# Values of batch 1 issued after the last keys of batch 0 have landed: a fused attention and expert kernel on one core

## The chip, the cores and the metric

The kernel runs on one core of one Trainium2 chip. The metric is the time of one execution on the device in microseconds (us); the kernel before takes 200.95 us, the median of 3 runs (200.51 to 201.13).

## What is computed

Attention over pooled keys and values, then a mixture of experts on its output. There are 8 batches, 8 heads, 576 rows of queries, keys and values with 64 columns, and 8 experts (512 to 1024 to 512).

```python
k_p = k.reshape(B, H, Sp, pool, D).mean(axis=3)      # pool = 8, Sp = 72
v_p = v.reshape(B, H, Sp, pool, D).mean(axis=3)
scores = scale * np.matmul(q, k_p.transpose(0, 1, 3, 2))
attn = softmax(scores)
x = np.matmul(attn, v_p)                             # to rows of 512
...
logits = xn @ en.T / tau                             # cosine router
expert_idx = np.argmax(logits, axis=1)
h = np.maximum(x[mask] @ w1[e], 0.0)                 # for each expert e
out[mask] = gate_w[mask, None] * (h @ w2[e])
```

## The kernel before

Each of the 8 batches goes through the same steps, and the steps of several batches run beside each other on the engines. Keys (`K`), values (`V`) and queries (`Q`) of a batch are loaded and cast to 16 bits by DMAs that GpSimd issues, 576 KB each as they land: `load_rows` (line 319) for keys and values, `load_q` (line 325) for queries. A load of keys or values has 72 rows of partitions. For batch 0 keys and values come in two DMAs each, 64 rows and then the last 8: `V0.0`, `V0.1`, `K0.0`, `K0.1`, and the queries in two halves, `Q0.0` and `Q0.1`. The values' mean gives a guess of the expert that the batch will use (`GM`, `GC`, `GL`, `GD`); `PK` reads that guess into a register of GpSimd (line 359), and then the expert's weights are loaded, 1024 KB each: `W1b` (line 343) and `W2b` (line 349). In the names the first digit behind the letters is the batch, except for weights: W10 is the first weight matrix for batch 0, W20 the second.

VectorE halves the values and keys three times (lines 448, 455, 462: `VA`, `VB`, `KA`, `KB`). For batch 0 alone TensorE sums the keys instead (line 472). VectorE transposes the queries (line 548), TensorE makes the scores (line 589), ScalarE the exponentials (597), TensorE the products with the values (634), VectorE normalizes (369, 370), TensorE transposes the result (378), then come the router and the two products with the weights (707, 719, 726). Matmuls of ones (814) keep TensorE at work in between early on. SyncE issues the stores of the output.

The order is not written by hand: `Plan.order` simulates the engines and the 16 DMA engines once, when the kernel is built, and picks the step that can start first; `TUNED` shifts priorities. For the loads the order is fixed by the list `LOADS`. Its beginning:

```python
LOADS = """
V0.0 V0.1 K0.0 K0.1 Q0.0 Q0.1 V1 PK0 W10 K1 Q1.0 W20 V2 PK1 W11 K2 Q2.0 V3 W21 V4 K3 PK2 W12
...
ROWS_DMA, Q_DMA, W_DMA = (12, 4.0, 1.2), (16, 2.85, 1.2), (16, 5.0, 2.2)
```

The second line of constants is the planner's own table of transfers: how many DMA engines a load of 72 rows, of queries and of weights is spread over, and the time that it assumes. The chosen order is emitted step by step. Each engine then runs its own instructions in that order, and waits on semaphores for data and for free buffers. There are two buffers each for keys, values and queries. All loads go through one software queue that GpSimd fills; the DMA engines work through it in order.

Some stores already wait for a late load on purpose: `note` records the instruction of a load under its name in `landing`, and `store` makes the store wait for it (`BEHIND`).

Of the kernel before, what the change touches and what calls it, by code (L numbers as in the profile page):

```python
# [106 lines left out]
class Plan:  # L107
# [5 lines left out]
    def add(self, name, engines, busy, prio, run, after=(), takes=(), uses=(), late=0.0,  # L113
            mode=None, tail=0.0):
        if isinstance(engines, str):
            engines = (engines,)
        if not isinstance(busy, tuple):
            busy = (busy,) * len(engines)
        s = Step(name, engines, busy, late, prio + TUNED.get(name, 0.0), [a for a in after if a], list(takes),
                 list(uses), run, mode, tail)  # L120
        for b in s.takes + s.uses:
            b.left += 1
        self.steps.append(s)
        self.by_name[name] = s
        return name
# [88 lines left out]
def kernel(  # L214
# [94 lines left out]
    def at_load(name):  # L309
        return -1000.0 + loads.index(name)  # L310
# [3 lines left out]
    def wire(dma, share=1.0):  # L314
        k, took, first = dma
        return k, took * share, first

    def load_rows(a, b, raw, g0=0, g1=G):
        return nc.gpsimd.dma_start(
            out=raw.rearrange("p h t d -> p h (t d)")[g0:g1],  # L320
            in_=a[b].rearrange("h (g t) d -> g h (t d)", g=G)[g0:g1])

    def load_q(b, qq, h0, n):
# [4 lines left out]
    landing = {}  # L328
    behind = dict(zip((f"S{t}" for b in range(B) for t in
                       [f"T{b}.{c}" for c in range(4)] + [f"L{b}"]), BEHIND))  # L330
    tails = {load: 0.34 if t[1] == "L" else 0.68 for t, load in behind.items()}

    def note(name, load):
        landing[name] = load.ins.name

    def store(name, eng, o, y):
        st = eng.dma_start(out=o, in_=y)
        if name in behind:
            tc.add_manual_dep(st.ins, landing[behind[name]], mybir.DependencyInfo(
                mybir.DependencyClass.Sync, mybir.DependencyReason.DATA), reason="late store")  # L340

    def load_w1(e_val, w1, cond=None):
        return nc.gpsimd.dma_start(
# [64 lines left out]
    def attention(b, base, xt):  # L408
# [3 lines left out]
        n = lambda s, *i: s + str(b) + "".join(f".{j}" for j in i)  # L412
# [4 lines left out]
        for c, src, raw in (("V", v, vr), ("K", k, kr)):  # L417
            if b == 0:
                add(n(c, 0), 'POOL', 0.9, at_load(n(c, 0)),
                    lambda src=src, raw=raw: load_rows(src, b, raw.tile, 0, 64),  # L420
                    takes=[raw], mode=(16, 2.78 if c == "V" else 2.7, 1.2), late=0.9)
                add(n(c, 1), 'POOL', 0.6, at_load(n(c, 1)),
                    lambda src=src, raw=raw: load_rows(src, b, raw.tile, 64),
                    uses=[raw], mode=(8, 1.25 if c == "V" else 0.3, 1.2), late=0.9)
            else:
                add(n(c), 'POOL', 0.8, at_load(n(c)),
                    lambda c=c, src=src, raw=raw: note(n(c), load_rows(src, b, raw.tile)),
                    takes=[raw], mode=wire(ROWS_DMA), tail=tails.get(n(c), 0.0), late=0.9)
        if b == 0:
            for i in range(NQ):  # L430
                add(n("Q", i), 'POOL', 0.8, at_load(n("Q", i)), lambda i=i: load_q(b, qq, i, 1),
                    takes=[] if i else [qq], uses=[qq] if i else [], mode=(16, 1.3 + i, 1.2), late=0.9)
        else:
            add(n("Q", 0), 'POOL', 0.8, at_load(n("Q", 0)), lambda: note(
                n("Q", 0), load_q(b, qq, 0, NQ)),
                takes=[qq], mode=wire(Q_DMA), tail=tails.get(n("Q", 0), 0.0), late=0.9)
# [30 lines left out]
        if b == 0:  # L467
# [14 lines left out]
            for a in range(NQ):  # L482
# [5 lines left out]
                    late=0.12)  # L488
# [3 lines left out]
        if b:  # L492
            add(n("KA"), 'DVE', 1.14, pr(-0.2), lambda: halve(kr.tile, 4),
                [n("K")] + (["XM0.4"] if b == 1 else []), uses=[kr],
                late=0.1)
            add(n("KB"), 'DVE', 1.08, pr(-0.2), k_fold, [n("KA")], takes=[kp], uses=[kr],
                late=0.1)
# [75 lines left out]
        else:  # L573
# [5 lines left out]
                late=0.1)  # L579
# [45 lines left out]
        for c in range(NC):  # L625
# [28 lines left out]
            def square(c=c, x=x):  # L654
# [9 lines left out]
                late=0.12)  # L664
# [77 lines left out]
    def ffn(b, base, xt):  # L742
        n = lambda s, *i: s + str(b) + "".join(f".{j}" for j in i)
        w1, w2 = Buf(w1_r[b % NW]), Buf(w2_r[b % NW])
        P = PERIOD
        add(n("PK"), 'POOL', 1.4, at_load(n("PK")), lambda: pick(b), [n("GD")])
        add(n("W1"), 'POOL', 0.8, at_load(n("W1")), lambda: note(
            n("W1"), load_w1(chosen[b], w1.tile, other(b))), [n("PK")], takes=[w1], mode=wire(W_DMA, 1.0 if b < NW else 1.0 - 1.0 / E), tail=tails.get(n("W1"), 0.0), late=0.9)
        add(n("W2"), 'POOL', 0.8, at_load(n("W2")), lambda: note(
# [21 lines left out]
        for c in range(4):  # L771
            p, y = Buf(bank, psum), Buf(y_r)
            f = base + P * (8 + 2 * c) / 17.0
            add(n("Y", c), 'PE', 1.73, f,
                lambda c=c, p=p: y_mm([h.tile for h in hT], w2.tile, c, p.tile[:, 0:DM]),
                [n("W2")] + hs,
                takes=[p], uses=[w2] + hT, late=0.22)
            add(n("YE", c), YE_ON, YE_BUSY, f - 2.0,
                lambda c=c, p=p, y=y: scale_rows(
                    y.tile, p.tile[:, 0:DM], g[:, c:c + 1], plan.by_name[n("YE", c)].on),  # L780
                [n("Y", c), n("ND")], takes=[y], uses=[p], late=0.12)
            add(n("ST", c), 'SP', 0.1, f, lambda c=c, y=y: store(
                n("ST", c), nc.sync, chunk_rows(o_b, c), y.tile), [n("YE", c), behind.get(n("ST", c))],
                uses=[y], mode=(0 if n("ST", c) in behind else 16, 0.68, 1.2), late=0.9)
# [19 lines left out]
    def put_last(o_b, y, name=""):  # L804
        for r in range(2):
            eng = nc.scalar if r and name == f"SL{B - 1}" else nc.sync
            store(name, eng, last_rows(o_b)[r], y[ts(r, 64), 0:DH])
# [171 lines left out]
    for b in range(B):  # L979
        xt = Buf(xt_r)  # L980
        attention(b, b * PERIOD, xt)
        ffn(b, (b + 1) * PERIOD, xt)
# [104 lines left out]
```

## Time and profile before

| | before |
|---|---|
| time, median of 3 | 200.95 us |
| the profiled execution | 201.33 us |
| its span, first to last instruction | 199.7 us |
| TensorE / VectorE / ScalarE / GpSimd busy | 95% / 70% / 68% / 22% |
| DMA moved | 38.71 MB, 194 GB/s over the span |

The profile is of one execution. Times in its rows are us from the start of the span. PE is TensorE's matmul, PEld its loading of weights, DVE VectorE, ACT ScalarE, POOL GpSimd, SP SyncE; a q behind an engine is its sequencer, which waits, reads registers and issues. L319 is line 319 of the kernel. Buffers' numbers are left out, so that `vr` is any buffer of raw values, `kr` of keys, `qq` of queries, `w` of weights. A matmul's end is modelled, so that neighbours seem to overlap.

### The profile page before, as it was taken

What the parts mean: (1) busy time and instruction counts of PE and PEld (TensorE: products, weight loads), DVE (VectorE), ACT (ScalarE), POOL (GpSimd) and SP (SyncE); (2) the same over time, 40 slices, a digit from 0 to 9 for tenths busy, and PEclk for the clock granted to TensorE, in tenths of its full rate; (3) what the DMA queues carried; (4) which work ended last, traced back from release to release, by engine and by line L of the source; (5) the groups of instructions that cost most, each with busy time, mean ns of one, the idle gap of its engine ahead of it and who ended that gap; (6) DMA issues with size and microseconds to landing.
All of it is one profiled execution on the core that took longest, in us unless ns stands there. A gap on an engine that the chain in (4) does not pass through costs nothing.

```text
span 199.7 us, 5353 instructions
## 1 busy us (share of the span) xinstructions
PE 188.9 (95%) x2080; PEld 124.1 (62%) x2081; DVE 140.1 (70%) x409; ACT 136.6 (68%) x313; POOL 43.0 (22%) x59
## 2 busy tenths in 40 slices
PE   7969999999999999999999999999999999999970
PEld 5854687547864676468666567566655677578430
DVE  2274699749997995688997997879997468241600
ACT  4016886768896979759867778469957988468430
POOL 7434025232204321035003500133000600002000
PEclk9999999999999999999999999999999999999997
DMA  3999999999999999999999999999997599990051
GB/s 49 172 191 199 207 211 197 195 200 205 210 188 190 214 209 192 212 209 227 247 168 213 214 252 233 222 179 242 247 218 245 128 217 216 229 335 22 25 190 34
DMA packets 27839, 38.71 MB, mean 194 GB/s; under 512 B 4248, under 2 KB 14488, under 8 KB 27808
## 3 DMA queue, kind: packets, MB, share of 16 engines
q0 software_dynamic: 21904, 28.85, 85.8%
q1 hardware_dynamic: 5824, 9.39, 13.8%
q8 instruction: 18, 0.29, 0.6%
q14 instruction: 13, 0.11, 0.2%
q10 hardware_dynamic: 80, 0.07, 0.1%
HBM read 61.88 MB, written 9.44 MB: 357 GB/s over the span
## 4 chain that ended last, share of the span: by engine, by line
PE 63%; DMA 22%; DVE 9%; issue 2%; POOL 1%; ACT 1%; DVEq 0%; POOLq 0%; ACTq 0%
DMA vr<-in_v_dram 22%; PE pb L707 21%; PE pb L719 17%; PE pa L589 4%; PE pb L814 4%; PE pa L719 3%; PE pa L707 3%; PE pa L634 3%; PE pb L378 3%; DVE vr L448 2%; PE pb L726 2%; DVE x L370 2%; PE pb L387 1%; DVE qT L548 1%; DVE kr L448 1%
## 5 line engine op out<-in xcount | busy, mean ns | idle before, releaser
L707 PE MATMUL pb<-xt,w 128*128 128x288 f16 (+2 forms) x432 | 61.3, 287 | 0.0
L707 PEld LDWEIGHTS <-w 128*128 128x128 f16 x512 | 47.1, 98 | 15.2 <-issue 4.6
L719 PE MATMUL pb<-w,hT 128*128 128x512 f16 x224 | 52.7, 379 | 0.0
L597 ACT ACTIVATE at<-pa 72x576 f16<-72x576 f32 (+2 forms) x64 | 38.3, 643 | 3.9 <-PE pa L589 3.5
L719 PEld LDWEIGHTS <-hT 128*128 128x128 f16 x256 | 23.2, 97 | 24.9 <-issue 1.3
L655 ACT ACTIVATE sq<-x 128x512 f16<-128x512 f16 x40 | 25.2, 631 | 13.2 <-DVE x L370 8.3
L713 ACT ACTIVATE hT<-pb 128x288 f16<-128x288 f32 (+2 forms) x74 | 28.6, 411 | 5.3 <-PE pb L707 3.3
L732 ACT ACTIVATE y<-pb,gm_all 128x512 f32<-128x512 f32 (+1 forms) x30 | 19.1, 635 | 14.7 <-PE pb L719 10.9
L370 DVE TENSOR_TENSOR x<-pa,r_all 128x512 f16<-128x512 f32 x38 | 26.3, 692 | 2.1
L548 DVE STREAM_TRANSPOSE qT<-qq 128x576 f16<-128x576 f16 x32 | 23.2, 754 | 1.0 <-DMA qq<-in_q_dram 1.0
L398 POOL TENSOR_TENSOR ssq_all<-ssq_all,half_c 128x5 f32<-128x5 f32 x8 | 10.3, 1294 | 50.5 <-ACT sq L655 50.5
L715 DVE TENSOR_SCALAR hT<-pb 128x288 f16<-128x288 f32 (+2 forms) x34 | 14.8, 446 | 6.5 <-PE pb L707 6.2
L349 POOL DMA_DIRECT2D w<-in_moe_w_dram x8 | 5.5, 688 | 64.3 <-PE pb L726 17.0
L814 PE MATMUL pb<-ones_m 128*128 128x256 f16 x102 | 16.4, 306 | 1.4 <-DVE half_c L821 1.4
L448 DVE TENSOR_TENSOR vr<-vr 72x2048 f16<-72x2048 f16 (+1 forms) x16 | 15.1, 941 | 2.2 <-DMA vr<-in_v_dram 2.1
L589 PE MATMUL pa<-qT,kpT 32*72 32x288 f16 (+2 forms) x256 | 15.6, 294 | 0.0
L378 PEld LDWEIGHTS <-x 128*128 128x128 f16 x160 | 10.9, 97 | 5.9 <-DVE x L370 1.9
L634 PEld LDWEIGHTS <-at 72*128 72x128 f16 x320 | 13.1, 98 | 1.9 <-issue 0.3
L378 PE MATMUL pb<-ident_h,x 128*128 128x128 f16 x144 | 13.4, 219 | 0.9 <-DVE x L370 0.7
L634 PE MATMUL pa<-vpx,at 72*128 72x65 f16 x304 | 14.2, 194 | 0.0
L650 ACT COPY xt<-pb 128x512 f16<-128x512 f16 (+1 forms) x25 | 13.0, 539 | 0.5 <-PE pb L378 0.3
L448 DVE TENSOR_TENSOR kr<-kr 72x2048 f16<-72x2048 f16 (+1 forms) x14 | 13.2, 941 | 0.0
(115 smaller groups left out, 197.2 us busy)
## 6 DMA issues: line engine op xcount, KB each, us to landing
w<-in_moe_w_dram POOLq DMA_DIRECT2D x16, 1024.0 KB, 15.9
out_dram<-y SPq DMA_DIRECT2D x32, 256.0 KB, 6.0
vr<-in_v_dram POOLq DMA_DIRECT2D x7, 576.0 KB, 21.3
kr<-in_k_dram POOLq DMA_DIRECT2D x7, 576.0 KB, 17.5
qq<-in_q_dram POOLq DMA_DIRECT2D x7, 576.0 KB, 15.6
out_dram<-y SPq DMA_DIRECT2D x15, 64.0 KB, 6.6
qq<-in_q_dram POOLq DMA_DIRECT2D x2, 288.0 KB, 9.6
vr<-in_v_dram POOLq DMA_DIRECT2D x1, 512.0 KB
```

Of the source, the lines that this page charges most:

```text
L370: nc.vector.tensor_tensor(out=x[:, ts(i, np_)], in0=pxv[:, :, 1:129].rearrange("p a (r d) -> p a r d", d=D), in1=rv.unsqueeze(3).to_broadc ...
L378: nc.tensor.transpose(out=pt.bitcast(FP16)[:, ts(w, 128)], in_=xf[:, ts(w, 128)], identity=ident_h)
L448: nc.vector.tensor_tensor(out=t[:, :, 0:m], in0=t[:, :, 0:m], in1=t[:, :, m:2 * m], op=ALU.add)
L548: nc.vector.transpose(out=qT.tile[:, a].rearrange("p t c e -> p (t c e)")[:, cols], in_=qq.tile[:, a, cols]),
L589: nc.tensor.matmul(out=tiles[m // 2].tile[0:gs, m % 2 * 512:m % 2 * 512 + (p1 - p0) * T], lhsT=kpT.tile[ts(m, R), a, c, 0:gs], rhs=qT.tile ...
L597: nc.scalar.activation(out=t.tile[:, :, p0 * T:p1 * T].rearrange("g r (p t) -> g r p t", t=T), in_=p.tile[0:G].rearrange("g (r c) -> g r c ...
L634: nc.tensor.matmul(out=px[h // 2 // np_].tile[:, o:o + 65], lhsT=at[h // 2].tile[:, h % 2, c0:c0 + 128], rhs=vp.tile[:, h // 2, 1 + h % 2 ...
L655: nc.scalar.activation(out=sq, in_=x.tile.rearrange("p a r d -> p (a r d)"), func=AF.Square, accum_out=ssq_all[:, b, c:c + 1])
L707: nc.tensor.matmul(out=p[:, 0:c1 - c0], lhsT=w1v[:, kk, w // 2, w % 2, :], rhs=xt[:, kk, c0:c1], start=(kk == 0), stop=(kk == 3))
L713: nc.scalar.activation(out=dst, in_=src, func=AF.Relu)
L719: landing[f"Y{c}"] = nc.tensor.matmul(out=p, lhsT=hT[w][:, ts(c, 128)], rhs=w2[:, w // 2, w % 2, :], start=(w == 0), stop=(w == 7))
L814: nc.tensor.matmul(out=p[:, 256:512], lhsT=ones_m[:, 0:128], rhs=ones_m[:, 0:256], start=True, stop=True)
```

## The change

`note` is now called for the second part of the loads of batch 0 too, so that `landing` knows `K0.1`. When V1 is noted, its DMA is made to wait until K0.1 has landed. The code that adds the wait moves from `store` into `wait_for`. The steps, their order and the planner's numbers are the same.

```diff
     tails = {load: 0.34 if t[1] == "L" else 0.68 for t, load in behind.items()}
 
+    def wait_for(ins, name):
+        tc.add_manual_dep(ins, landing[name], mybir.DependencyInfo(
+            mybir.DependencyClass.Sync, mybir.DependencyReason.DATA), reason="late transfer")
+
     def note(name, load):
         landing[name] = load.ins.name
+        if name == "V1":
+            wait_for(load.ins, "K0.1")
 
     def store(name, eng, o, y):
         st = eng.dma_start(out=o, in_=y)
         if name in behind:
-            tc.add_manual_dep(st.ins, landing[behind[name]], mybir.DependencyInfo(
-                mybir.DependencyClass.Sync, mybir.DependencyReason.DATA), reason="late store")
+            wait_for(st.ins, behind[name])
...
                 add(n(c, 1), 'POOL', 0.6, at_load(n(c, 1)),
-                    lambda src=src, raw=raw: load_rows(src, b, raw.tile, 64),
+                    lambda c=c, src=src, raw=raw: note(n(c, 1), load_rows(src, b, raw.tile, 64)),
                     uses=[raw], mode=(8, 1.25 if c == "V" else 0.3, 1.2), late=0.9)
```

## Rows read from the trace of the kernel before

**Rows 1.** The page: busy share of engines, HBM traffic, the last chain by engine.
```profile
PE 188.9 (95%) x2080; PEld 124.1 (62%) x2081; DVE 140.1 (70%) x409; ACT 136.6 (68%) x313; POOL 43.0 (22%) x59
...
HBM read 61.88 MB, written 9.44 MB: 357 GB/s over the span
...
PE 63%; DMA 22%; DVE 9%; issue 2%; POOL 1%; ACT 1%; DVEq 0%; POOLq 0%; ACTq 0%
```

**Rows 2.** The chain that ended last, in time: start, length, what.
```profile
16.19 22.43 DMA vr<-in_v_dram
...
40.63 0.43 DVE vpx L462
41.35 21.27 DMA vr<-in_v_dram
```

**Rows 3.** Timeline of VectorE: start, length, line, operation; idle time before and its releaser.
```profile
26.19 1.21 DVE L448 TENSOR_TENSOR vr<-vr 72x2048 f16<-72x2048 f16 x1
...
43.71 0.21 DVE L369 RECIPROCAL r_all<-pa 128x8 f32<-128x8 f32 x1 [2.66 <-PE pb L505]
...
62.64 1.22 DVE L448 TENSOR_TENSOR vr<-vr 72x2048 f16<-72x2048 f16 x1 [1.24 <-DMA vr<-in_v_dram]
```

**Rows 4.** The chain once more, where TensorE takes it over.
```profile
70.63 0.40 PE pb L378 x4
```

**Rows 5.** Timeline of GpSimd: its issues of loads.
```profile
1.46 1.47 POOL L319 DMA_DIRECT2D vr<-in_v_dram  x2 [0.84 <-POOLq L1068]
...
6.23 0.89 POOL L319 DMA_DIRECT2D vr<-in_v_dram  x1
13.09 0.79 POOL L343 DMA_DIRECT2D w<-in_moe_w_dram  x1 [5.98 <-DVE vpx L462]
...
32.30 0.82 POOL L343 DMA_DIRECT2D w<-in_moe_w_dram  x1 [2.85 <-DVE lmax_all L393]
```

**Rows 6.** DMA issues up to 7 us: size, us from issue to landing.
```profile
vr<-in_v_dram POOLq DMA_DIRECT2D x1, 576.0 KB, 12.0
...
kr<-in_k_dram POOLq DMA_DIRECT2D x1, 64.0 KB, 8.5
```

**Rows 7.** Sums of keys on TensorE (timeline); GpSimd's read of the guess (by line).
```profile
12.14 1.92 PE L472 MATMUL pb<-kr,ident_h 72*128 72x256 f16 x16 [1.09 <-DMA kr<-in_k_dram]
...
L359 POOLq TENSOR_LOAD <-ix_all x1: 480/480/480, 11.6 to 11.6; - x1
```

**Rows 8.** Stretches: length, busy by engine, clock; DMA share and GB/s stand last.
```profile
0.00:12.00 12.00, 9.68 (x123) 7.23 (x124) 4.16 (x21) 2.02 (x4) 5.79 (x15) 1.00 0.84 126
...
14.50:15.00 0.50, 0.48 (x6) 0.44 (x7) 0.20 (x2) 0.24 (x1) 0.50 (x2) 1.00 1.08 154
5.00:6.00 1.00, 1.00 (x6) 0.73 (x5) 0.85 (x4) 0.00 (x0) 1.00 (x3) 1.00 1.23 205
2.80:3.00 0.20, 0.20 (x3) 0.15 (x1) 0.00 (x0) 0.20 (x1) 0.20 (x2) 1.00 0.00 0
3.00:3.10 0.10, 0.10 (x3) 0.05 (x1) 0.00 (x0) 0.10 (x1) 0.10 (x1) 1.00 1.48 51
3.00:4.50 1.50, 1.50 (x9) 1.06 (x7) 0.00 (x0) 0.37 (x2) 1.41 (x4) 1.00 0.80 84
6.50:9.50 3.00, 3.00 (x74) 2.58 (x76) 0.17 (x1) 0.00 (x0) 0.62 (x1) 1.00 1.15 157
...
34.00:36.00 2.00, 2.00 (x22) 1.01 (x21) 1.92 (x7) 1.90 (x5) 2.00 (x3) 1.00 1.06 168
```

**Rows 9.** W10, W20: us from issue (at 15.43 for W20) to landing; their first matmuls.
```profile
DMA to landing us min/median/max: 10.5/10.5/10.5
...
25.65 0.60 PE L707 MATMUL pb<-xt,w 128*128 128x256 f16 x4
...
DMA to landing us min/median/max: 20.0/20.0/20.0
...
37.05 1.89 PE L719 MATMUL pb<-w,hT 128*128 128x512 f16 x8
```

## Prediction

> **What bounds the kernel now.** I read the page first: TensorE is busy for 95% of the span, yet only 63% of the chain that ended last lies on TensorE, and 22% on one kind of transfer, the load of values [rows 1]. The chain in order of time says which: V2 from its issue at 16.19 to 38.6, and V4 from 41.35 to 62.6 [rows 2]. Neither transfer takes 22 us by itself; each stands in GpSimd's DMA queue behind what was issued before it. So up to 62.6 the kernel is paced by that queue, and after it by TensorE. The timeline of VectorE shows where the two landings bite. After V2 it has 2.66 us of idle time before its next normalization, so V2 has room; at V4 it stands idle for 1.24 us until the transfer lands, and starts the first halving of V4 at once [rows 3]. From there VectorE works without a gap until the normalization that TensorE's transposes at 70.63 need, and from 70.63 the chain is TensorE's [rows 4]. The question is therefore: what does the change do to the time at which V4 lands?
>
> **The moved step.** V1 is issued at 6.23 today, when nobody waits for it: it lands 12.0 us later, at 18.2, and is first read at 26.19 [rows 3, 5, 6]. What the early issue buys is that V1 stands ready behind the first queries. The last rows of the first keys, K0.1, land 8.5 us after their issue, at about 12.1: the first sums over keys wait for that landing and start at 12.14 [rows 6, 7]. So the new wait bites, by 5.9 us. Once V4's buffer was free at 41.06, with the last fold of V2, GpSimd began V4's issue at 41.35, 0.29 later [rows 2]; counted from 12.1 that puts V1's issue at 12.4.
>
> **What is queued behind the wait.** On GpSimd, in program order: the read of the guessed expert (today at 11.6), W10, K1, Q1, W20, V2. Nothing else of GpSimd lies between 6.2 and 13.1, and the store queue of SyncE isn't touched. The read of the expert comes 1.49 us before W10 today [rows 5, 7]; behind V1 it starts at 12.1 and W10 goes out at about 13.6 instead of 13.09, and K1 to V2 by the same 0.5 later. At the earliest W10 follows V1's 0.89 us of issuing, 13.3: the delay is 0.2 to 0.5. Those issues stand before a queue that is full, and cost something only where an engine runs dry.
>
> **Where the queue runs dry.** This is the term that counts. Values and keys of batch 0 and its two halves of queries are 3 x 576 KB = 1.77 MB (V1 has the size of each) [rows 6]. Up to 12.0 the engines had moved 126 GB/s x 12 us = 1.51 MB; the other 0.26 MB at 205 GB/s take 1.25 us. So the average DMA engine finishes the first queries at 13.25 [rows 8]. Today V1 follows without a pause. From V0's issue at 1.46 to the first packet (none up to 3.0, then 51 GB/s) pass 1.54 to 1.64 us [rows 5, 8]; from 12.4 that gives V1's first packet at 14.0. **The hole is 14.0 - 13.25 = 0.75 us** on the average engine that carries V1. Its upper end: after the very first issue the engines reached only 84 GB/s over 1.5 us where 205 is the pace, 0.89 us lost in starting [rows 8]. With all of that the hole is 1.64. Its lower end: what lands is set by the last engine. V1 at its pace of 154 GB/s takes 3.83 us from 13.25, to 17.1, but lands at 18.2. If the other 1.1 us are engines that lag, the last one still has queries to load until 14.35 and loses nothing; if they are the completion's own delay, it loses all. I take 0.75, the average engine without a slow start: V1 restarts engines that have just worked, nearer to the steady row than to the first issue's.
>
> One figure of the Trainium skill speaks against the trace here: "DMA: Bandwidth & Descriptors", section Specifications, gives about 1 us to the first byte for a transfer that GpSimd issues. By it V1's first packet would come at 13.4, the hole would be 0.15 and the time about 201.1; the row of V0 shows 1.54 at least, and I go by the row.
>
> **What the hole costs.** The queue works in order, so whatever comes after V1 is late by the hole until some stretch has time to spare. W10 lands at 23.6 and is first used at 25.65, W20 at 35.4 and is used at 37.05: 2.0 and 1.6 us to spare [rows 9]. V1 has 8 us, V2 the 2.66 us behind its halving. V4 has nothing: VectorE already waits for it. One place might give time back: from 34 to 36 the engines moved 168 GB/s, because W11 went out only at 32.30 and some of them ran empty; that is 2 x (1 - 168/205) = 0.36 us on average [rows 5, 8]. Engines with V1 and V2 on them are not among the empty ones, so I take nothing off and keep 0.36 for the range. V4 then lands at 63.4, VectorE's unbroken work moves by 0.75, TensorE's transposes by as much, and the rest follows them.
>
> **Sum.** 0 (V1, W10 to V2 behind slack) + 0.75 (V4's landing, passed on whole) = +0.75 us. The profiled execution took 201.33 us, its span 199.7; it becomes 202.1 and 200.4. Against the median of 200.95 the forecast is **201.7**.
>
> **Rivals.**
> *A. The hole is not passed on.* The last engine is busy with queries until 14.35, or the stretch at 34 to 36 gives the time back: 0 to 0.4, about 201.1. For it: the 1.1 us between V1's last packet by the average and its landing; against it: V4 needs several engines, and those that end soonest now lose most.
> *B. V1 in the queue slows what is ahead of it, and the wait ends that: faster.* From 6.5 to 9.5, just after V1's issue, the engines moved 157 GB/s against 205 before: 3 x (1 - 157/205) = 0.70 us [rows 8]. If V1's presence did that, keys and first queries land 0.70 earlier, batch 0 and the whole queue with them. It decides if the hole then stays below 0.70; with the hole gone as in A the time is 200.95 - 0.70 = 200.25. Against it: the issues of W10 to V2 stand in the queue in the same way without such a dip, and where V1 runs alone at 14.5 to 15.0 it moves 154 GB/s, 0.75 of 205. That is what 12 engines of 16 give (the 72 rows divide by 12, as the kernel's own table of transfers has it): each engine keeps its pace, and V1 takes nothing from engines that still load queries [rows 8].
> The Trainium skill, "DMA: Bandwidth & Descriptors", section Specifications, puts a limit of about 358 GB/s on a core's share of HBM, and this kernel averages 357 [rows 1]. By that rule V1's first packets would slow the last queries and B would gain; the row at 14.5 speaks for a limit by engine, so B's chance stays small.
> *C. The change does nothing*, because K0.1 is there before V1's turn: excluded by 12.1 against 6.23.
>
> **How the numbers follow.** The forecast (hole passed on, 0.4 to 1.6) has 0.55, A 0.33, B 0.12. About 0.3% (0.6 us) is what a measurement of this kernel can tell from no change. Of the forecast's 0.55 some 0.07 lie below 0.6, so slower 0.48, same 0.33 + 0.07 = 0.40, faster 0.12. The range goes from 200.6, which leaves out most of B, up to 200.95 + 1.64 = 202.6.
>
> **What would show it.** In the changed profile: V1's issue at 12.4 and W10's at 13.6; in the stretches from 13 to 15 a drop of GB/s below 150; V1 landing at about 18.9; V4 at 63.4, VectorE's wait before it 2.0 instead of 1.24; the transposes at 71.4 instead of 70.63; and no other new wait. I am wrong in the hole if V1's first packet comes before 13.5 or after 14.5; wrong in the passing on if V1 lands 0.75 later and V4 doesn't; B is right if the rate from 6.5 to 9.5 rises to 205 and K0.1 lands near 11.4.

## The result and the profile after

| | before | after |
|---|---|---|
| time, median of 6 runs each | 200.73 us (200.19 to 201.43) | 202.44 us (201.98 to 202.66) |
| ratio, 95% interval | | 1.008 (1.0056 to 1.0105) |
| the profiled execution, its span | 201.33, 199.7 us | 202.24, 200.6 us |
| V1: issue, landing | 6.23, 18.2 | 11.61, 19.0 |

The change makes the kernel slower, by 0.8%: 1.1 to 2.1 us, 1.6 in the middle. The forecast was 201.7 and the range 200.6 to 202.6. The direction and the mechanism held, the size did not: the loss is about twice the 0.75 us of the forecast.

From line 343 on, lines of the kernel after have numbers five higher: L348 is W10's load (before L343), L383 the transposes (378), L453 the halving (448), L724 the second product (719).

The page of the kernel after: busy time by engine, HBM traffic, the chain by engine.

```profile
PE 189.5 (94%) x2080; PEld 124.1 (62%) x2081; DVE 140.2 (70%) x409; ACT 136.7 (68%) x313; POOL 43.1 (21%) x59
...
HBM read 61.88 MB, written 9.44 MB: 355 GB/s over the span
...
PE 61%; DMA 25%; DVE 4%; ACT 3%; issue 2%; POOL 1%; SPq 0%; POOLq 0%; DVEq 0%; ACTq 0%
```

Work and bytes are what they were; the chain has more of the transfers and less of TensorE [rows 1]. In order of time (start, length, what) it runs over the same two loads as before [rows 2]. V2 lands 2.1 us later (40.75 for 38.62); V4 is issued 2.1 later and lands 1.0 later (63.63 for 62.62):

```profile
16.40 24.35 DMA vr<-in_v_dram
40.77 1.23 DVE vr L453
43.47 20.16 DMA vr<-in_v_dram
```

The timeline of GpSimd after (start, length, line, operation, idle time before and its releaser) shows that the wait bites, and that W10 goes out only 0.2 us later than before [rows 5]:

```profile
11.61 0.87 POOL L319 DMA_DIRECT2D vr<-in_v_dram  x1 [5.35 <-DMA kr<-in_k_dram]
13.29 0.79 POOL L348 DMA_DIRECT2D w<-in_moe_w_dram  x1 [0.81 <-DVE vpx L467]
```

**A second execution of before.** The unchanged kernel was profiled once more (200.19 us, span 198.5). What was expected of it:

> The kernel before once more, for a second profile of it. If the landing of K0.1 at 12.1 and the rate of 157 GB/s from 6.5 to 9.5 belong to V1's early issue, they stand here again (12.1 and about 157). If they differ from one execution to the next, K0.1 lands at 11.3 to 11.6 as in the changed kernel.

The execution of the rows ahead of the prediction was a late one in its first 13 us. K0.1 took 8.5 us to land there [rows 6], 7.6 in the second execution, and 7.7 after the change. Over all fourteen executions profiled here it is 7.5 to 7.8 in nine and 8.2 to 8.5 in five. The late ones are four of the nine in which V1, or a part of it, went out by 9.3, and one of the five in which it went out at 11.0 or later; that is too few to tell whether V1 has a part in it. After is compared with the second execution of before, whose K0.1 landed as early as its own.

The stretches around V1 (length, then busy time by engine, clock; DMA share and GB/s last), first of the second execution of before:

```profile
6.50:9.50 3.00, 3.00 (x79) 2.61 (x78) 0.17 (x1) 0.00 (x0) 0.61 (x1) 1.00 1.17 183
12.50:13.00 0.50, 0.50 (x7) 0.36 (x4) 0.50 (x1) 0.00 (x0) 0.01 (x1) 1.00 1.17 215
13.00:13.50 0.50, 0.18 (x2) 0.00 (x0) 0.19 (x1) 0.28 (x2) 0.50 (x1) 1.00 1.07 160
13.50:14.00 0.50, 0.36 (x5) 0.33 (x6) 0.08 (x1) 0.36 (x2) 0.50 (x2) 1.00 1.08 173
14.00:14.50 0.50, 0.50 (x8) 0.45 (x7) 0.50 (x2) 0.00 (x0) 0.50 (x1) 1.00 1.02 154
14.50:15.00 0.50, 0.50 (x6) 0.34 (x4) 0.50 (x3) 0.00 (x0) 0.50 (x2) 1.00 1.62 168
16.00:17.50 1.50, 1.46 (x14) 0.54 (x12) 0.62 (x1) 1.43 (x4) 0.95 (x2) 1.00 1.16 202
15.00:19.50 4.50, 4.46 (x45) 1.75 (x43) 1.58 (x4) 3.73 (x7) 1.95 (x3) 1.00 1.09 195
```

and then of after:

```profile
6.50:9.50 3.00, 3.00 (x63) 2.49 (x64) 0.18 (x1) 0.00 (x0) 0.00 (x0) 1.00 1.18 179
12.50:13.00 0.50, 0.50 (x7) 0.46 (x5) 0.50 (x2) 0.00 (x0) 0.00 (x0) 1.00 0.82 162
13.00:13.50 0.50, 0.30 (x3) 0.01 (x1) 0.50 (x1) 0.17 (x1) 0.21 (x1) 1.00 1.18 67
13.50:14.00 0.50, 0.24 (x4) 0.24 (x5) 0.02 (x1) 0.47 (x2) 0.50 (x1) 1.00 0.27 28
14.00:14.50 0.50, 0.50 (x8) 0.45 (x7) 0.47 (x2) 0.00 (x0) 0.50 (x2) 1.00 0.96 85
14.50:15.00 0.50, 0.50 (x9) 0.43 (x6) 0.50 (x3) 0.00 (x0) 0.50 (x2) 1.00 0.77 121
16.00:17.50 1.50, 1.46 (x14) 0.51 (x12) 0.73 (x2) 1.46 (x3) 1.25 (x2) 1.00 1.15 175
15.00:19.50 4.50, 4.46 (x45) 1.66 (x43) 1.70 (x5) 3.71 (x6) 2.25 (x3) 1.00 1.08 167
0.00:13.00 13.00, 11.50 (x138) 8.72 (x140) 4.93 (x23) 2.02 (x4) 5.80 (x15) 1.00 0.86 137
```

This is the hole, and it has two parts. The queue runs out of work: 137 GB/s x 13 us are 1.78 MB, so the average engine is through with the 1.77 MB ahead of V1 at about 12.9, and the first packets of V1's size come at 13.2. And V1 starts slowly: 28, 85 and 121 GB/s from 13.5 to 15.0, where 154 is its pace [rows 8]. The first part is about 0.3 us, so most of the hole is the second. Summed from 12.5 to 15.0 the difference is 407 GB/s x 0.5 us = 204 KB. It goes on growing behind that: from 15.0 to 19.5 another (195 - 167) x 4.5 = 126 KB are missing, while V1's end and W10's beginning are loaded. Together 330 KB are 1.6 us of all engines at 205 GB/s, close to the 1.8 us by which V1 lands later.

**Where the hole comes out.** TensorE of the second execution of before, the first product with W20 and the transposes that answer to [rows 4, 9]:

```profile
36.16 1.89 PE L719 MATMUL pb<-w,hT 128*128 128x512 f16 x8
...
69.90 0.40 PE L378 MATMUL pb<-ident_h,x 128*128 128x128 f16 x4
```

and of after:

```profile
37.25 1.89 PE L724 MATMUL pb<-w,hT 128*128 128x512 f16 x8 [0.81 <-DMA w<-in_moe_w_dram]
...
66.61 0.40 PE L383 MATMUL pb<-ident_h,x 128*128 128x128 f16 x4 [0.41 <-DVE x L375]
...
69.83 0.40 PE L383 MATMUL pb<-ident_h,x 128*128 128x128 f16 x4 [0.36 <-DVE x L375]
...
71.86 0.40 PE L383 MATMUL pb<-ident_h,x 128*128 128x128 f16 x4
```

At 37.25 TensorE is 1.09 us later than before, because W20 has not landed: it lands 21.6 us after its issue at 15.64, at 37.2, where before it landed at 15.33 + 20.0 = 35.3. That distance stays the same up to 65.8. Then it grows, at the two marked waits for VectorE, to 71.86 - 69.90 = 1.96, and the spans end 2.1 apart. VectorE shows why; of before, and then of after:

```profile
61.20 1.22 DVE L448 TENSOR_TENSOR vr<-vr 72x2048 f16<-72x2048 f16 x1 [0.68 <-DMA vr<-in_v_dram]
63.00 0.21 DVE L369 RECIPROCAL r_all<-pa 128x8 f32<-128x8 f32 x1 [0.58 <-PE pa L634]
...
64.83 1.22 DVE L448 TENSOR_TENSOR kr<-kr 72x2048 f16<-72x2048 f16 x1
```

```profile
43.91 0.21 DVE L374 RECIPROCAL r_all<-pa 128x8 f32<-128x8 f32 x1 [0.74 <-PE pb L510]
...
63.65 1.22 DVE L453 TENSOR_TENSOR vr<-vr 72x2048 f16<-72x2048 f16 x1 [2.04 <-DMA vr<-in_v_dram]
...
66.80 1.22 DVE L453 TENSOR_TENSOR kr<-kr 72x2048 f16<-72x2048 f16 x1 [0.24 <-DMA kr<-in_k_dram]
```

V4 is halved 2.45 us later, more than the hole (from 44 to 50 the engines moved 193 GB/s, before 207); of this 1.09 was lost already at W20. Of the other 1.36 before had 0.58 to spare in this execution, since VectorE stood idle for TensorE behind the halving. K3, just behind V4, is waited for as well. V2 is harmless: after its halving VectorE still has 0.74 us to spare [rows 3]. So the hole of the first 20 us is paid at two places, 1.09 us at W20 and 0.87 at V4 and K3. (The two profiled executions lie 2.05 us apart, the medians 1.7; the six of before reach from 200.19 to 201.43.)

### The profile page after: what moved, and what is told of

It is laid out like the page before. It is cut to its first block, busy times and chain, and to the rows that moved or that the text cites. A ratio compares the mean times of both kernels' runs of the same rounds, so it can differ in the third digit from the quotient of the medians.

```text
span 200.6 us, 5353 instructions
## 1 busy us (share of the span) xinstructions
PE 189.5 (94%) x2080; PEld 124.1 (62%) x2081; DVE 140.2 (70%) x409; ACT 136.7 (68%) x313; POOL 43.1 (21%) x59
## 4 chain that ended last, share of the span: by engine, by line
PE 61%; DMA 25%; DVE 4%; ACT 3%; issue 2%; POOL 1%; SPq 0%; POOLq 0%; DVEq 0%; ACTq 0%
DMA vr<-in_v_dram 22%; PE pb L712 21%; PE pb L724 16%; PE pb L819 4%; PE pa L594 4%; PE pa L724 3%; DMA out_dram<-y 3%; PE pa L712 3%; PE pa L639 3%; PE pb L383 2%; DVE vr L453 2%; PE pb L731 2%; PE pb L392 1%; ACT y L737 1%; ACT sq L660 1%
## 5 line engine op out<-in xcount | busy, mean ns | idle before, releaser
L724 PE MATMUL pb<-w,hT 128*128 128x512 f16 x224 | 52.7, 379 | 0.8 <-DMA w<-in_moe_w_dram 0.8
L724 PEld LDWEIGHTS <-hT 128*128 128x128 f16 x256 | 23.2, 97 | 25.9 <-issue 2.3
L737 ACT ACTIVATE y<-pb,gm_all 128x512 f32<-128x512 f32 (+1 forms) x30 | 19.0, 634 | 15.7 <-PE pb L724 11.8
L453 DVE TENSOR_TENSOR vr<-vr 72x2048 f16<-72x2048 f16 (+1 forms) x16 | 15.1, 942 | 5.9 <-DMA vr<-in_v_dram 5.8
L383 PE MATMUL pb<-ident_h,x 128*128 128x128 f16 x144 | 13.7, 220 | 1.7 <-DVE x L375 1.4
L383 PEld LDWEIGHTS <-x 128*128 128x128 f16 x160 | 10.9, 98 | 7.0 <-DVE x L375 3.5
L453 DVE TENSOR_TENSOR kr<-kr 72x2048 f16<-72x2048 f16 (+1 forms) x14 | 13.2, 943 | 0.5 <-DMA kr<-in_k_dram 0.5
```

Source lines behind the costliest of these rows:

```text
L383: nc.tensor.transpose(out=pt.bitcast(FP16)[:, ts(w, 128)], in_=xf[:, ts(w, 128)], identity=ident_h)
L453: nc.vector.tensor_tensor(out=t[:, :, 0:m], in0=t[:, :, 0:m], in1=t[:, :, m:2 * m], op=ALU.add)
L724: landing[f"Y{c}"] = nc.tensor.matmul(out=p, lhsT=hT[w][:, ts(c, 128)], rhs=w2[:, w // 2, w % 2, :], start=(w == 0), stop=(w == 7))
```

## The experiments

Ratios are of runs taken in turn with the kernel before, so they need not equal the quotient of the medians. The diffs show the line that matters; beside it, loads that a wait names are noted under their names. Each profile is of one execution, which need not be a typical one of its kernel.

**Is it the wait, or the time of the issue?** V1 waits for a transfer that is there early.

```diff
-            wait_for(load.ins, "K0.1")
+            wait_for(load.ins, "V0.1")
```

> V1 waits for the last rows of the first values (V0.1, landing at about 8.2) instead of the keys'. It is issued at about 8.5, first packet at about 10.1, well before the first queries are through at 13. Theory of the hole (V1 comes too late behind the queries, DMA engines run empty, V4 lands late): no hole, 200.7 within 0.4, V4 lands as in the kernel before. Rival that the wait itself or the moved issue costs: still about 202.4. Rival that V1's presence in the queue slows the keys: K0.1 lands 0.3 to 0.8 earlier than 12.1 and the time is 200.3 or less.

Measured: 200.64, ratio 0.9997 (0.9964 to 1.0031). V1 goes out at 8.51, 2.3 us later than before. Its DMA row (size, us from issue to landing) and the stretch in which after had 67 GB/s:

```profile
vr<-in_v_dram POOLq DMA_DIRECT2D x1, 576.0 KB, 8.9
```

```profile
13.00:13.50 0.50, 0.23 (x3) 0.00 (x0) 0.48 (x1) 0.23 (x1) 0.22 (x1) 1.00 1.03 152
```

The wait itself costs nothing that the interval of 0.3% could show. It gives nothing either: from 6.5 to 9.5 the engines move 184 GB/s, with V1 in the queue from 8.5 on, 179 in after without it, and 183 in the second execution of before, so taking V1 out of the queue does not speed up the keys.

**A wait that ends later.** `Q0.0` instead of `K0.1` (and the halves of the queries are noted too).

```diff
-            wait_for(load.ins, "K0.1")
+            wait_for(load.ins, "Q0.0")
```

> V1 waits for the first half of the first queries (Q0.0, landing at about 12.7 to 13.5). Issued about 1.5 later than in the changed kernel, first packet at about 14.7. Theory of the hole: the hole grows by about 1.4, so does the landing of V4: 203.8 within 0.5. Rival that only the later issues of W10 to V2 cost, which have 1 to 2 us to spare: not above 202.8.

Measured: 203.17, ratio 1.0105 (1.0032 to 1.0177), just under what the theory of the hole expected and above the rival. The issue (duration, first and last start) with its landing, and a stretch behind it:

```profile
L319 POOL DMA_DIRECT2D vr<-in_v_dram x1: 876/876/876, 13.5 to 13.5; - x1
...
DMA to landing us min/median/max: 7.4/7.4/7.4
```

```profile
14.50:15.00 0.50, 0.50 (x8) 0.45 (x7) 0.49 (x2) 0.00 (x0) 0.04 (x1) 1.00 0.00 0
```

V1 went out at 13.48, and from 14.5, when the last queries are through, up to 15.0 no engine moves anything: at least 1.5 us pass from the start of the issue to the first packet. The Trainium skill, "DMA: Bandwidth & Descriptors", section Specifications, gives about 1 us for that; counted from the start of the issue, this row decides against it. The landing comes 7.4 us after the issue, as in after. Against after V1 lands 1.9 us later, and the medians are 0.7 apart: not all of a larger hole is passed on.

**V1 early, W10 late.** V1 has no wait; W10 waits for the second half of the queries, so that the queue runs dry one load later (the halves of the queries are noted here too).

```diff
-        if name == "V1":
-            wait_for(load.ins, "K0.1")
+        if name == "W10":
+            wait_for(load.ins, "Q0.1")
```

> V1 is issued at once, as in the kernel before; instead W10 waits for the second half of the first queries (landing at about 15.3), so W10, K1, Q1, W20 and V2 go out about 2.4 later than before and 2.2 later than in the changed kernel. Theory of the hole: 12 of 16 DMA engines have V1 until about 17.2, and W10's first packet comes at about 17.5, so the queue loses 0.3 to 0.6 on those: 201.0 to 201.4. Rival that the later issues behind V1 are what costs: 203 or more, above the changed kernel's 202.4.

Measured: 201.83, ratio 1.0047 (1.0011 to 1.0082), so 0.9 us slower: between the two expectations and nearer to that of the hole. W10 goes out at 15.10 instead of 13.0, while V1 still keeps its engines at 156 to 160 GB/s up to 16. Then comes a hole of its own:

```profile
16.00:17.50 1.50, 1.46 (x14) 0.53 (x12) 0.70 (x2) 1.44 (x3) 1.50 (x3) 1.00 0.91 103
```

103 GB/s over 1.5 us instead of 202. So the hole is not something that belongs to V1: W10 issued late leaves one too. Where the 0.9 us are lost is not shown. The profiled execution was the fastest of the ten, 200.57 us; TensorE did not wait for W20 in it, and its transposes came at 70.28, 0.38 later than before:

```profile
36.27 1.89 PE L724 MATMUL pb<-w,hT 128*128 128x512 f16 x8
```

**Filling the hole.** 24 of V1's 72 rows go out at once, the other 48 wait for K0.1 as in after. If only the empty queue cost time, the first third should cover it.

```diff
+        cut = 24 if name == "V1" else 0
+        if cut:
+            load_rows(src, int(name[1:]), raw, 0, cut)
+        note(name, load_rows(src, int(name[1:]), raw, cut))
...
```

> V1 in two DMAs: its first 24 rows are issued at once, as before (1.3 us of work for 12 DMA engines), the other 48 rows wait for K0.1 as in the changed kernel, and W10 goes out behind them. Theory of the hole: the 24 rows fill the time until the late part's first packet at about 13.5, and V4 lands within 0.4 of the kernel before: 200.9 within 0.4. Rival that the wait and the later issues cost: 202.4, as the changed kernel.

Measured: 202.26, ratio 1.0036 (0.9991 to 1.0081). Its profiled execution had late first queries, so one more was profiled:

> The kernel with V1 in two DMAs once more, for a second profile: in its first one the first half of the first queries landed late, at 15.0. If that belongs to the split, it lands at 15 again. If it was this one execution, it lands at 12.2 to 13.5, and what is left of the loss is the split's own.

That execution took 202.69. The timeline of GpSimd, the DMA row of the late part and the stretch of W10:

```profile
11.46 0.65 POOL L319 DMA_DIRECT2D vr<-in_v_dram  x1 [4.54 <-DVE ix_all L535]
```

```profile
vr<-in_v_dram POOLq DMA_DIRECT2D x1, 384.0 KB, 6.8
```

```profile
16.00:17.50 1.50, 1.46 (x14) 0.54 (x12) 0.57 (x1) 1.43 (x4) 0.90 (x2) 1.00 1.00 96
```

The queries were on time in this one, so their lateness was the first execution's own. The theory of the hole failed in this profile. The queue no longer runs dry at 13 to 14 (171 and 169 GB/s), yet the late part takes 6.8 us to land, 0.6 less than the whole of V1 in after for two thirds of its bytes, and W10 starts at 96 GB/s instead of 202. TensorE does not wait for W20 here; instead VectorE waits for the queries Q2:

```profile
51.99 0.78 DVE L559 STREAM_TRANSPOSE qT<-qq 128x576 f16<-128x576 f16 x1 [1.43 <-DMA qq<-in_q_dram]
```

So a load can be slow although the engines do not stand empty before it. Two things keep this from being a proof: a DMA of 48 rows is not the one of 72, and W10 itself was not late here (12.94, before 12.99), so its 96 GB/s are not explained by its own issue. How much the split really costs is left open: the interval reaches from no change to that of after.

**Where the loss is passed on.** If V4 were the only place, relieving the queue just ahead of V4 should make before and after equal. W21, the load in front of V4, fetches only a quarter of its 1024 KB, and the rest of its buffer is set to zero.

```diff
-            n("W2"), load_w2(chosen[b], w2.tile, other(b))), ...
+            n("W2"), (load_quarter if b == 1 else load_w2)(chosen[b], w2.tile, other(b))), ...
```

Expected of before with this cut, and of after with it:

> The kernel before, but W21 loads only a quarter of the matrix (256 KB for 1024 KB; the rest is zero, so batch 1's second product is not the reference's). 768 KB less stand in the queue ahead of V4: V4 lands about 3.7 earlier, at 59, and nobody waits for it. Time 199.5 to 200.7.

> The changed kernel with the same quarter of W21 (batch 1's second product is not the reference's). Theory that the cost reaches the end only through the landings of V4 and K3: nobody waits for these here, and the time is that of the quartered kernel before within 0.4. Rival that it reaches the end on another way (V2's landing, W10, TensorE's order): 1.2 to 1.7 more than the quartered kernel before.

Measured: 200.49 (ratio to before 0.9999, 0.9977 to 1.002) and 201.43 (1.0054, 1.0025 to 1.0082). They do not become equal: 0.9 us remain, about half of the loss. TensorE's first product with W20, before with the cut and after with it, and VectorE's halving of V4 in the latter:

```profile
36.22 1.89 PE L726 MATMUL pb<-w,hT 128*128 128x512 f16 x8
```

```profile
36.76 1.89 PE L731 MATMUL pb<-w,hT 128*128 128x512 f16 x8 [0.49 <-DMA w<-in_moe_w_dram]
```

```profile
61.05 1.21 DVE L460 TENSOR_TENSOR vr<-vr 72x2048 f16<-72x2048 f16 x1
```

Nobody waits for V4 any more, so that half has gone; what remains arises at W20: there the two traces are 0.54 us apart, and still 0.58 at the transposes (70.38 and 69.80). To check that, the same cut was made to W20 itself (b == 0), which takes 768 KB, 3.8 us at 205 GB/s, out of the queue ahead of both places:

> The kernel before, but W20 loads only a quarter of the matrix (256 KB for 1024 KB; the rest is zero, so batch 0's second product is not the reference's). The queue is 3.7 us shorter from W20 on: W20 lands at about 31.5, V2 at 35, V4 at 57.5, and nobody waits for any of them. 199.9 to 200.7.

> The changed kernel with the same quarter of W20 (batch 0's second product is not the reference's). Theory that the late queue reaches TensorE only in two places, W20's landing and the landings of V4 and K3: both are cut here, and the time is that of its partner with the quartered W20 within 0.3. Rival that some third way exists: 0.6 or more above the partner.

Measured: 200.78 (0.9991, 0.9958 to 1.0025), just above what was expected, and 201.01 (1.0016, 0.9979 to 1.0052). The difference of 0.2 us can't be told from none, though the interval leaves room for up to 1.0. In after with this cut the product with W20 starts without a wait, and VectorE waits for V4 no longer than in the second execution of before:

```profile
36.06 1.89 PE L731 MATMUL pb<-w,hT 128*128 128x512 f16 x8
...
61.18 1.22 DVE L460 TENSOR_TENSOR vr<-vr 72x2048 f16<-72x2048 f16 x1 [0.76 <-DMA vr<-in_v_dram]
```

The expectation that V4 would land at 57.5 and nobody would wait for it failed. The queue, now shorter, runs dry ahead of W11, which goes out only at 31.31 (138 GB/s from 32 to 34). V4 therefore lands no earlier, but the lateness of the first 20 us ends there too. So the runs bear out the two places found by comparing the traces; a small third one is not excluded.

**The empty queue, or the late issue?** V1 waits for `K0.0` instead of `K0.1`, and goes out 0.6 us earlier than in after, so that its first packets should meet the last of the queries and the queue not run dry.

```diff
-            wait_for(load.ins, "K0.1")
+            wait_for(load.ins, "K0.0")
...
```

> V1 waits for the first 64 rows of the first keys (K0.0, landing at about 10.8) instead of the last 8 (about 11.3): issued at about 11.0, first packet at about 12.6, just before the engines are through with the first queries at 13.0. Theory that the loss is engines that stand empty and then start slowly: nothing stands empty, at most 0.3 us of it is left, 200.7 to 201.2. Rival that V1 starts slowly whenever it is issued shortly before it is due, empty engines or not: most of the loss stays, V1 lands at 18.3 or later and the time is 201.7 or more.

Measured: 202.17, ratio 1.0061 (1.002 to 1.0102). The rival held: still slow. V1 went out at 11.01; its DMA row, two stretches, and TensorE's wait at W20:

```profile
vr<-in_v_dram POOLq DMA_DIRECT2D x1, 576.0 KB, 7.4
```

```profile
13.00:13.50 0.50, 0.33 (x4) 0.05 (x1) 0.47 (x1) 0.13 (x1) 0.50 (x1) 1.00 0.63 61
...
12.50:13.50 1.00, 0.83 (x8) 0.50 (x6) 0.78 (x1) 0.13 (x1) 0.69 (x1) 1.00 0.61 72
```

```profile
37.25 1.89 PE L724 MATMUL pb<-w,hT 128*128 128x512 f16 x8 [0.76 <-DMA w<-in_moe_w_dram]
```

Up to 12.5 the engines had moved 140 GB/s x 12.5 us = 1.75 of the 1.77 MB ahead of V1, and V1's first packets came at 12.6, so the average engine was not left without work; yet in the next 1 us the engines were busy for only 0.61 of the time. The slow start comes without an empty queue in front of it.

Issues at 11.0, 11.6 and 13.5, and at 11.4 in the two kernels with the wait and a quartered load: each time V1 lands 7.4 us later. Without delay it lands at 17.2 in the second execution of before (6.23 + 11.0). So, as an estimate, an issue should be free up to about 17.2 - 7.4 = 9.8.

**A point between.** No wait; five small operations of GpSimd stand in front of V1's issue.

```diff
+        for _ in range(5 if name == "V1" else 0):
+            nc.gpsimd.iota(spare, pattern=[[1, 512]], base=0, channel_multiplier=0,
+                           allow_small_or_imprecise_dtypes=True)
...
```

> The kernel before without any wait; five dummy iotas on GpSimd ahead of V1 put its issue off to about 10.0 (9.5 to 10.5), and W10 goes out as before. In the runs so far V1 landed at 17.2 to 17.5 when issued at 6.2 to 8.5, and 7.4 us after its issue when issued at 11.0, 11.4, 11.6 and 13.5. Theory that a late load has its whole time from issue to landing ahead of it, whatever stands before it: it lands at the later of 17.3 and issue + 7.4, 17.4 at an issue of 10.0, and the time is 200.7 to 201.2. Rival that only the wait makes V1 slow, or that any issue after 8.5 costs the whole: V1 lands at 18.2 or later, 201.7 or more; or, without the wait, at 17.3 even when issued at 10.5.

The issue came out somewhat earlier than meant; the timeline of GpSimd and the DMA row:

```profile
9.29 0.88 POOL L320 DMA_DIRECT2D vr<-in_v_dram  x1
```

```profile
vr<-in_v_dram POOLq DMA_DIRECT2D x1, 576.0 KB, 8.6
```

It lands at 17.9, behind queries that were 0.6 us late in this execution, and the rate from 13.0 to 15.0 stays at 156 to 172 GB/s: no slow start. Measured: 201.34, ratio 1.003 (1.001 to 1.0051), a little above the expectation. In the transfer 9.3 is still free, as 9.8 would have it; in the time 0.2 to 1.0 us are lost, and why was not found. The profiled execution, 200.81, does not show the loss, and whether the five added operations cost something by themselves was not tested. Where between 9.3 and 11.0 the slow start sets in is open.

## Why the prediction was right and wrong

**The wait bites: right.** GpSimd stands idle for 5.35 us. V1's issue was put at 12.4 and came at 11.61; the 12.1 for K0.1 [rows 6] was that one execution's.

**What is queued behind the wait: right.** W10 was to go out 0.2 to 0.5 later; it was 0.2 (0.3 against the second execution), since the read of the expert came at 11.8, beside V1's issue and not behind it. No new wait arose from it.

**The hole: the step that failed.** "I take 0.75, the average engine without a slow start: V1 restarts engines that have just worked, nearer to the steady row than to the first issue's." The 0.75 was empty queue alone, and the slow start stood at nothing. After shows the reverse: the average engine was without work for about 0.3 us, V1 started slowly although the engines had just worked (85 and 121 GB/s), and its landing moved by 1.8 us, from 17.2 to 19.0. V1's first packet at 13.2 is also earlier than the 13.5 that the prediction named as a sign against its hole. The range held because its upper end, 1.64, had taken the slow start in. All the parts stood in the prediction: 1.55 to the first packet, 0.89 of slow start, 3.83 at V1's pace, 1.1 from there to the landing. Added from the issue they make 7.4, the very time that five kernels measured, and 11.6 + 7.4 = 19.0. I subtracted instead from the moment at which the average engine runs out of queries, and so took the slow start as something that a short hole would spare. V1's forecast landing, 18.9, was close only because the issue was put 0.8 too late and the transfer taken 0.9 too short.

**What the hole costs: half right.** V4 passes a delay on, through VectorE to the transposes: right. That it has no slack at all was true of the first execution; the second had 0.58 us. That the times came close to those foreseen (V4 63.6 for 63.4, VectorE's wait 2.04 for 2.0, the transposes 71.86 for 71.4) is in part luck: they were counted from the late execution, in which V4 was halved at 62.64 [rows 3] and not at 61.20. W10 and V2 did have room. W20 did not have the 1.6 us that I read from [rows 9]: its 35.4 was the landing, but the product at 37.05 belonged to an execution whose first batch was late by 0.9. In the second execution of before W20 lands at 35.3 as well, and is used at 36.16: 0.85 to spare. A hole of 0.75 would have fitted into that, one of 1.8 does not, and W20 became the first place where TensorE stands still. "No other new wait" was wrong for this reason. The slack of 34 to 36 gave nothing back that reached V4. The loss is about as large as the hole, but not because one place passes it on whole, as in the forecast's sum: it is 1.09 at W20 and 0.87 at V4 and K3.

**Rival A (not passed on)** fell: the landing moves by more than the average engine's hole, so the last engine isn't spared. **Rival B (V1 slows the keys)** fell: 183 GB/s from 6.5 to 9.5 with V1 in the queue, 179 with V1 held back; the 157 of [rows 8] was the late execution. **Rival C** was rightly excluded.

Open is why a late load starts slowly. The runs show that it does, for V1 and for W10, and V1 behind K0.0 shows it with no empty queue on the average engine ahead of it.

## What to carry to other kernels

A load that nobody waits for yet is not idle in the queue: it is what lets the engines go on without a pause. Before delaying an issue, add the load's whole time from issue to landing, with the start, and compare it with the landing that it has today; what is left over is the room, here by estimate 9.8 - 6.2 = 3.6 us. An issue at 9.3 bore that out in its landing, though not wholly in its time. Slack of one or two us, read from a single execution, should be checked in a second one (W20's was read as 1.6 and was 0.85 there), above all where an early stretch shows a rate that nothing explains.

## What the hardware showed beside this

A 576 KB load of 72 rows issued at 11.0, 11.4, 11.6 or 13.5 lands 7.4 us later each time. At 8.5 and 9.3 it takes longer, 8.9 and 8.6, but behind a full queue, and the rate from 13 to 15 does not fall. In these runs a late issue costs the load's fixed time from issue to landing. The Trainium skill, "DMA: Bandwidth & Descriptors", section Rules for kernel authors, advises to issue early and wait late because the setup then overlaps; the runs agree, and show where early ends: an issue at 8.5 gives the same time as one at 6.2, one at 11.0 costs 0.6%. The 0.3% at 9.3 is not explained.

The first transfers of an execution vary by themselves. K0.1 took 7.5 to 8.5 us to land over fourteen executions, and what follows it in the first batch is late by as much.
